# A third buffer for late outputs, and loads, stores and visits moved on one SyncE queue

## The chip, the cores and the metric

The kernel runs on one NeuronCore of one Trainium2 chip. The metric is the device time of one execution in microseconds; three unprofiled runs of the kernel before were taken, and one more execution with the hardware profiler, from which the trace comes.

## The reference

Windowed attention over 8 batches of 576 tokens, 8 heads of 64, followed by a dense softplus layer pair. Half of the heads see the last 32 keys, the other half every fourth of the last 128.

```python
scores = scale * np.matmul(q, k.transpose(0, 1, 3, 2))          # q, k, v: (8, 8, 576, 64)
mask_plain = (rel >= 0) & (rel < 32)
mask_dil = (rel >= 0) & (rel < 128) & (rel % 4 == 0)
attn = softmax(np.where(masks, scores, -1e9))
x = np.matmul(attn, v) as (4608, 512)
h = x @ w_in                                                     # (4608, 2048)
g = np.maximum(h, 0.0) + np.log1p(np.exp(-np.abs(h)))
return g @ w_out                                                 # (4608, 512)
```

## The kernel before

The 4608 tokens are nine chunks c of 512 columns. For each chunk the attention gives x (512 by 512), the first product gives h in 16 blocks ff of 128 rows, the softplus makes g, and the second product sums all 16 blocks into four PSUM banks o0 to o3 (m = 0 to 3). Every float32 operand is held as a high and a low part, so each product is three matmuls. Chunks 0 and 1 run in an opening stage written out as a list of words and in `slots` (one time unit is one slot: one block's h and one block's o). Chunks 2 to 8 run in a late stage: two blocks at a time take seven steps (`h_x`, `h_y`: a seven-product scheme on sums of x and weights), with about one quarter of a block's o between two steps. One round of seven steps is one `n`; its length in the trace is 10.55 us.

Attention of the chunks from 2 on is done two groups at a time, in visits that lie between the other PE work: `scores` (128 small matmuls into `s_ps`), then on DVE the maximum, on ACT the exponentials, on POOL the division, a DVE transposition `sq` that goes out to DRAM (`turned`) and comes back as `pt`, and then `values` (128 small matmuls into `a_ps` from `pt` and `v`). Its rows are turned by DVE, stored (`rows`) and read back as `x_full`.

The order is set by hand: `at(when, part)` puts a part at a time in slots, `step(n, k, part)` at a step of the late stage, and a heap hands them out; each engine then runs its instructions in the order in which they were written. `attend` places one visit of the opening stage, `attend_late(i)` visit i of eleven in the late stage, where scores come at step `begun` = 28i + 5 (plus `LATER_S[i]`) and values at `ended` = 28i + 28 + `LATER_V[i]`. Nearly all DMAs are issued by SyncE (SP, line 138) in the written order, and a DMA that has to wait holds back all behind it.

Two things touch DRAM beside loads and results. The opening stage leaves half-summed outputs of chunks 0 and 1 there (`kept`), which come back as `ob`. It also copies the 16 decoded blocks of `w_out` there (`keep_w_out`), since the SBUF that holds them is taken for other factors; the late stage loads them back, two 256 KB tiles `t` for each block.

`finished` closes a late chunk: for each m it copies the bank to one of the two halves of `ob` (m even on DVE, m odd on ACT) and stores that (`out_t`, 256 KB). So m = 2 takes the half of m = 0, and m = 3 that of m = 1. The bank is free for the next chunk's sum when its copy is done.

Of the kernel before, what the change touches and what calls it, by code (L numbers as in the profile page):

```python
# [14 lines left out]
F32 = mybir.dt.float32  # L15
# [9 lines left out]
P = 128  # L25
# [3 lines left out]
CH = 512  # L29
# [11 lines left out]
NPR = H // 2  # L41
# [4 lines left out]
FIRST = 2  # L46
# [49 lines left out]
def tile_windowed_attention_softplus_ffn(  # L96
# [13 lines left out]
    const = ctx.enter_context(tc.tile_pool(name="const", bufs=1))  # L110
# [9 lines left out]
    slots, at = [], {0: 0, 1: 0}  # L120
# [10 lines left out]
    def pin(ins):  # L131

        tc.keep_in_program_order(ins)
# [3 lines left out]
    def load_dma(engine=None, **kw):  # L137
        ins = tc.keep_in_program_order((engine or nc.sync).dma_start(**kw))  # L138
        if engine is None and len(under_way) < THIN:
            if len(under_way) >= DEPTH:  # L140
                tc.add_manual_dep(
                    ins.ins,
                    under_way[-DEPTH].ins.name,
                    mybir.DependencyInfo(mybir.DependencyClass.Sync, mybir.DependencyReason.DATA),
                    reason="at most so many of the first loads under way",
                )
            under_way.append(ins)
# [54 lines left out]
    def matmul(**kw):  # L202
        tc.keep_in_program_order(nc.tensor.matmul(**kw))  # L203

    def bank(name, tag):
        return psum.tile([P, CH], F32, name=name, tag=tag, bufs=2 if tag == "h" else 1)
# [422 lines left out]
    def at(when, part, *what, cost=0.0):  # L629
        heapq.heappush(events, (when, next(serial), cost, part, what))  # L630
# [169 lines left out]
    for word in OPENING.split():  # L800
        name = word[:3] if word[0] == "D" and word[1] != "l" else word.rstrip("0123456789_")
# [105 lines left out]
    def load_w_out(u):  # L907
        if u < len(uses):
            loaded[u] = [rest(2 * (u % 3) + part) for part in range(2)]
            for part in range(2):  # L910
                load_dma(out=loaded[u][part].bitcast(F32), in_=w_out[uses[u][1], :, part])

    def attend(n, when, lag):

        at(when, scores, n, cost=-1.45)
        for e in range(2):
            g, then = groups[n + e], when + e
            at(then + 0.12, g.maximum, cost=1.34)
            at(then + 0.37, g.exponentials)
            at(then + 1.0, g.divisor, cost=0.36)  # L920
            at(then + 1.0, g.divide)
            at(then + 1.37, turn, n + e, cost=0.65)
            at(then + 1.5, send, n + e)
            at(then + 2.2, bring, n + e)
        at(when + 3.3, load_v, n + 1)
        at(when + 3.45, load_queries, n + 2)
        at(when + lag, values, n, cost=-1.45)
        for e in range(2):
            at(when + lag + 0.25 + 0.25 * e, groups[n + e].turn_rows, cost=0.65)
        at(when + lag + 0.7, groups[n].send_x)  # L930
        at(when + lag + 1.25, groups[n].bring_x)
        at(when + lag + 0.01, load_keys, n + 2)
        at(when + lag + 1.3, load_v, n + 2)

    def decoding(keys):

# [19 lines left out]
    for p in range(EARLY):  # L956
        early += [((20.5, 20.5, 20.5, 20.5, 22.5)[p], *chore) for chore in chores_of(p)]
    for ff in range(NFF):
        at(18 + 0.55 * ff, keep_w_out, ff)
    for j in range(2):  # L960
        attend(FIRST * NPR + 2 * j, 10.2 + 7.5 * j, 4.125)
    attend((FIRST + 1) * NPR, 26.7, 4.6)
    at(26.2, ob_tiles, 0, True)
    for n in range(4):
        at(26 + 0.2 * n, combine, FIRST, n, cost=0.69)
# [6 lines left out]
    def step(n, k, part, *what, cost=0.0, after=0):  # L972

        at(LATE + 2 * n + STEP * (k + 0.9) + 0.001 * after, part, *what, cost=cost)
# [13 lines left out]
                step(n, 1, split_low, c, name, cost=0.7)  # L988

    LATER_S = (1, 0, 0, 1, 0, 0, 0, -1, 2, 1, 0)  # L990
    LATER_V = (0, -1, 2, 0, 0, 0, 0, 0, 0, 0, 3)

    def attend_late(i):

        n = (FIRST + 1) * NPR + 2 + 2 * i
        begun, ended = 28 * i + 5, 28 * i + 28 + LATER_V[i]

        def by(k, part, *what, cost=0.0, after=0):
            step(*divmod(k, 7), part, *what, cost=cost, after=after)

        by(begun + LATER_S[i], scores, n, after=1, cost=-1.45)
        for e in range(2):
            g, then = groups[n + e], begun + 7 * e
            late = 0 if e else max(LATER_S[i], 0)
            by(then + 1 + late, g.maximum, cost=1.34)
            by(then + 2 + late, g.exponentials, after=3)
            late = late // 2
            by(then + 6 + late, g.divisor, cost=0.36)
            by(then + 6 + late, g.divide)
            by(then + 8 + late, turn, n + e, cost=0.65)  # L1010
            by(then + 8 + late, send, n + e, after=4)
            by(then + 11 + late, bring, n + e)
        by(begun + 17, load_v, n + 1)
        by(begun + 20, load_queries, n + 2)
        by(ended, values, n, after=1, cost=-1.45)
        by(ended, load_keys, n + 2, after=2)
        for e in range(2):
            by(ended + 1 + e, groups[n + e].turn_rows, cost=0.65)
        by(ended + 3, groups[n].send_x, after=3)
        by(ended + 6, groups[n].bring_x, after=3)  # L1020
        by(ended + 8, load_v, n + 2, after=2)

    chores = []
    for c in range(FIRST + 1, NCH):
        n = (c - 1 - FIRST) * NPAIR
# [12 lines left out]
    for i in range(11):  # L1038
        attend_late(i)
# [30 lines left out]

    banks = [bank(f"h_{n}", "h") for n in "xy"]
    temps = const.tile([P, 3, HALF], F32, name="temps", tag="xl11")
    outs = []
    hs = {}

    def product(p, name, x, b, first):
# [30 lines left out]
        step(n + 1, 5 if second else 2, g_low, i, cost=0.69)  # L1107

    def finished(m, c, src):
        dst = outs[0][:, m % 2]  # L1110
        if m % 2:
            pin(nc.scalar.copy(out=dst, in_=src))  # L1112
        else:
            pin(nc.vector.tensor_copy(out=dst, in_=src))
        load_dma(out=out[m * P : (m + 1) * P, c * CH : (c + 1) * CH], in_=dst)

    def late_o(u, m, half=None):
        c, ff = uses[u]
        gh, gl = ready[len(slots) + u]
        first, final = ff == 0, ff == NFF - 1  # L1120
        if first and m == 0:
            for k in range(NKT):
                o_ps[k] = bank(f"o_ps{k}", f"o{k}")
        cols = slice(0, CH) if half is None else slice(half * HALF, (half + 1) * HALF)
        ws = slice(m * P, (m + 1) * P)
        for j, (part, gg) in enumerate(((0, gh), (0, gl), (1, gh))):
            matmul(
                out=o_ps[m][:, cols], lhsT=loaded[u][part][:, ws], rhs=gg[:, cols],
                start=first and j == 0, stop=(final or u == len(uses) - 2) and j == 2,
                skip_group_check=half is not None,  # L1130
            )
        if half is not None:
            return
        if final:
            if not outs:
                outs.append(const.tile([P, 2, CH], F32, name="ob", tag=f"w{NFF - 1}_1"))
            at(now[0] + (1 + (m == 2)) * STEP, finished, m, c, o_ps[m], cost=0.0 if m % 2 else 0.69)
        if m == NKT - 1:
            load_w_out(u + 3)

    pending = [(o_part, i, m) for i in range(len(slots) - LAG, len(slots)) for m in range(NKT)]
    pending += [(late_o, u, m) for u in range(len(uses) - 1) for m in range(NKT)]

    def outputs(n):
# [21 lines left out]
    for n, (c, p) in enumerate((c, p) for c in range(FIRST, NCH) for p in range(NPAIR)):  # L1166
        u = 2 * n
        for k, (x, weights, b, first, to, temp) in enumerate(steps):
# [10 lines left out]
            while chores and chores[0][:2] <= (n, k) and behind + chores[0][2] < 0.4:  # L1179
                _, _, cost, chore = chores.pop(0)  # L1180
# [8 lines left out]
    for half in range(2):  # L1189
        ob = const.tile([P, NKT, HALF], F32, name="pt", tag=("s", "v")[half])  # L1190
        for m in range(NKT):
            late_o(len(uses) - 1, m, half)
            src = o_ps[m][:, half * HALF : (half + 1) * HALF]
            if m % 2:
                nc.vector.tensor_copy(out=ob[:, m], in_=src)
            else:
                nc.scalar.copy(out=ob[:, m], in_=src)
            cols = slice(at_out + half * HALF, at_out + (half + 1) * HALF)
            if half and m > 1:
                engine = nc.sync if m % 2 else nc.scalar  # L1200
                engine.dma_start(out=out[m * P : (m + 1) * P, cols], in_=ob[:, m])
            elif m % 2:
                nc.sync.dma_start(
                    out=out[(m - 1) * P : (m + 1) * P, cols].rearrange("(m p) n -> p m n", p=P),
                    in_=ob[:, m - 1 : m + 1],
                )
# [120 lines left out]
```

## Time and profile before

| | |
|---|---|
| unprofiled runs | 885.37, 880.83, 882.01 us; median 882.01 |
| profiled execution | 885.35 us; its span 883.6 us |
| mean granted TensorE clock | 0.980 |
| busy share of the span | PE 97%, PEld 84%, DVE 70%, ACT 60%, POOL 4% |
| DMA | 168.81 MB, mean 191 GB/s |
| median from issue to landing | `t` 3.2 us, `v` 4.5 us, `w_out` store 5.8 us, `out_t` 2.4 us |

PE is busy nearly all of the time, so what can be won lies in the few places where it stands still, and those have to be looked for one by one. "Busy" counts modelled ends of pipelined matmuls. In a timeline row, the bracket at the end tells how long the engine was idle before the row and what ended that; "issue" means that no semaphore of the profile did. The chain of waits names at each moment the work that the end of the program hung on.

### The profile page before, as it was taken

The numbers are of one execution on the slowest core, as the hardware profiler recorded it, in microseconds if no ns is written. First come the engines' busy times: TensorE is split into PE (matmuls) and PEld (weight loads), VectorE is DVE, ScalarE is ACT, GpSimd is POOL, SyncE is SP. The second block draws the span as 40 slices with busy tenths as digits, with TensorE's granted clock in tenths as the row PEclk, the third lists the DMA queues.
The fourth block names the chain that finished last, engine by engine and source line by source line (L and its number), as shares of the span: only waits on it lengthen the run. The fifth ranks groups of instructions, "written<-read, shape, count | busy, mean of one in ns | idle before, by whom it ended". The sixth has DMA issues, their size and how long they took to land.

```text
span 883.6 us, 22785 instructions
## 1 busy us (share of the span) xinstructions
PE 856.5 (97%) x9143; PEld 739.5 (84%) x9143; DVE 618.5 (70%) x1260; ACT 533.0 (60%) x1327; POOL 31.6 (4%) x34
## 2 busy tenths in 40 slices
PE   6799999999999999999999999999899999999998
PEld 4578888787888988888788988898789888899897
DVE  5598898887888886576655776576647675675444
ACT  5587778766565756466554656565646564465443
POOL 0000000000000100000000000000000000000000
PEclk6699999999999999999999999999999999999999
DMA  9849445782757476666665665655575765434223
GB/s 328 299 132 365 182 133 183 259 297 79 214 193 222 162 217 198 198 186 209 206 190 187 183 215 187 220 175 190 174 217 168 215 192 173 135 105 144 96 97 118
DMA packets 107305, 168.81 MB, mean 191 GB/s; under 512 B 11072, under 2 KB 41920, under 8 KB 107200
## 3 DMA queue, kind: packets, MB, share of 16 engines
q1 hardware_dynamic: 106480, 166.18, 57.9%
q8 instruction: 72, 1.18, 0.6%
q10 hardware_dynamic: 720, 1.18, 0.4%
q14 instruction: 33, 0.27, 0.1%
HBM read 132.71 MB, written 34.60 MB: 189 GB/s over the span
## 4 chain that ended last, share of the span: by engine, by line
PE 85%; DMA 5%; ACT 4%; DVE 3%; issue 2%; SPq 0%; POOL 0%; ACTq 0%; DVEq 0%; POOLq 0%
PE o_ps L203 40%; PE h_x L203 17%; PE h_y L203 13%; PE h_ps L203 7%; PE a_ps L203 3%; PE s_ps L203 3%; DMA out_t<-ob 2%; ACT s L421 2%; DMA t<-w_out 1%; DMA ob<-kept 1%; DMA raw<-w 1%; PE t_ps L450 1%; DMA v<-vp 0%; SPq L138 0%; ACT ob L1112 0%
## 5 line engine op out<-in xcount | busy, mean ns | idle before, releaser
L203 PE MATMUL o_ps<-gh,t 128*128 128x512 f32 (+1 forms) x904 | 344.0, 393 | 6.1 <-ACT ob L1112 6.1
L203 PEld LDWEIGHTS o_ps<-gh,t 128*128 128x128 f32 x904 | 170.7, 189 | 29.4 <-ACT ob L1112 7.8
L666 ACT ACTIVATE e<-hs 128x512 f32<-128x512 f32 x112 | 70.0, 625 | 187.4 <-DVE hs L1098 187.3
L203 PE MATMUL o_ps<-gl,t 128*128 128x512 f32 (+1 forms) x452 | 179.1, 396 | 0.0
L685 ACT CAST gh<-e 128x512 fp32r<-128x512 f32 x140 | 86.3, 617 | 58.1 <-DVE e L673 56.6
L691 DVE TENSOR_TENSOR gl<-e,gh 128x512 fp32r<-128x512 f32 x144 | 102.4, 711 | 8.6 <-ACT gh L685 8.0
L203 PEld LDWEIGHTS h_x<-a,parts 128*128 128x128 f32 x672 | 96.1, 191 | 10.5 <-DVE temps L1096 0.4
L203 PEld LDWEIGHTS h_y<-s,t 128*128 128x128 f32 x672 | 94.3, 188 | 10.1 <-DVE temps L1098 0.2
L203 PE MATMUL h_x<-a,parts 128*128 128x256 f32 x672 | 99.7, 285 | 0.0
L203 PE MATMUL h_y<-s,t 128*128 128x256 f32 x672 | 98.8, 283 | 0.0
L668 ACT ACTIVATE e<-e 128x512 f32<-128x512 f32 x144 | 91.1, 633 | 4.6
L667 ACT ACTIVATE e<-e 128x512 f32<-128x512 f32 x144 | 91.1, 632 | 4.6
L203 PEld LDWEIGHTS o_ps<-gl,t 128*128 128x128 f32 x452 | 86.9, 192 | 2.9 <-DVE gl L691 0.4
L203 PE MATMUL h_ps<-xh,parts 128*128 128x512 f32 x256 | 89.0, 403 | 0.1
L203 PE MATMUL o_ps<-gh,parts 128*128 128x512 f32 x256 | 87.5, 394 | 1.0 <-DVE ob L746 1.0
L1098 DVE TENSOR_TENSOR hs<-h_x,temps 128x256 f32<-128x256 f32 x112 | 47.3, 422 | 58.0 <-PE h_x L203 57.6
L421 ACT ACTIVATE s<-s,nm 128x64 f32<-128x64 f32 x224 | 74.8, 335 | 9.7 <-DVE nm L413 9.6
L1098 DVE TENSOR_TENSOR temps<-h_y,temps 128x256 f32<-128x256 f32 x112 | 47.3, 423 | 46.0 <-PE h_y L203 45.5
L673 DVE SCALAR_TENSOR_TENSOR e<-hs,e 128x512 f32<-128x512 f32 x112 | 76.3, 681 | 2.1 <-ACT e L668 1.8
L1096 DVE COPY temps<-h_x 128x256 f32<-128x256 f32 x56 | 23.7, 422 | 57.2 <-PE h_x L203 57.1
L203 PEld LDWEIGHTS h_ps<-xh,parts 128*128 128x128 f32 x256 | 49.1, 192 | 11.3 <-DVE e L673 1.1
L203 PEld LDWEIGHTS o_ps<-gh,parts 128*128 128x128 f32 x256 | 48.1, 188 | 12.0 <-DVE ob L746 1.7
(82 smaller groups left out, 1195.2 us busy)
## 6 DMA issues: line engine op xcount, KB each, us to landing
t<-w_out SPq DMA_DIRECT2D x224, 256.0 KB, 3.2
raw<-w SPq DMA_DIRECT2D x64, 256.0 KB, 5.6
v<-vp SPq DMA_DIRECT2D x28, 512.0 KB, 4.5
q<-qp SPq DMA_DIRECT2D x36, 256.0 KB, 5.0
w_out<-parts SPq DMA_DIRECT2D x16, 512.0 KB, 5.8
out_t<-ob SPq DMA_DIRECT2D x32, 256.0 KB, 2.4
turned<-sq SPq DMA_DIRECT2D x112, 64.0 KB, 2.4
pt<-turned SPq DMA_DIRECT2D x28, 256.0 KB, 2.8
```

Source lines behind the costliest of these rows:

```text
L203: tc.keep_in_program_order(nc.tensor.matmul(**kw))
L421: pin(nc.scalar.activation(out=self.blocks[:, t], in_=src, func=AF.Exp, bias=self.nm[:, t : t + 1], scale=1.0 / 8.0 if self.masked else 1. ...
L450: nc.tensor.transpose(out=self.turned_to[:, m * P : (m + 1) * P], in_=self.s[:, m * P : (m + 1) * P], identity=ident,)
L666: pin(nc.scalar.activation(out=e, in_=tiles[i], func=AF.Abs))
L667: pin(nc.scalar.activation(out=e, in_=e, func=AF.Exp, scale=-1.0))
L668: pin(nc.scalar.activation(out=e, in_=e, func=AF.Ln, bias=1.0))
L673: pin(nc.vector.scalar_tensor_tensor(out=e, in0=tiles.pop(i), scalar=0.0, in1=e, op0=ALU.max, op1=ALU.add))
L685: pin((copy or nc.scalar.copy)(out=gh, in_=ready[i]))
L691: pin(nc.vector.tensor_tensor(out=gl, in0=e, in1=gh.bitcast(F32), op=ALU.subtract))
L1096: pin(nc.vector.tensor_copy(out=dst, in_=src))
L1098: pin(nc.vector.tensor_tensor(out=dst, in0=src, in1=temps[:, temp], op=ALU.add))
```

## The change

- `finished` hands out three buffers in turn (`stores` counts copies over all chunks): the two halves of `ob` and a new tile `third`.
- `load_v` of a late visit comes at step `begun` + 40 in place of `ended` + 8, that is nine steps later (one or two more where `LATER_V` was negative, fewer where it was positive). In the third opening visit it comes 1.1 slots later.
- `keep_w_out` of blocks 4 to 15 comes at 22.4 to 26.8 slots instead of 20.2 to 26.25.
- `LATER_V` of late visits 1 and 9 is one step lower: their values come one step earlier.
- In the third opening visit, the first group's maximum and exponentials come a quarter of a slot later.

```diff
-    def attend(n, when, lag):
+    def attend(n, when, lag, wait=0.0):
...
-            at(then + 0.12, g.maximum, cost=1.34)
-            at(then + 0.37, g.exponentials)
+            late = 0 if e else wait
+            at(then + 0.12 + late, g.maximum, cost=1.34)
+            at(then + 0.37 + late, g.exponentials)
...
-        at(when + lag + 1.3, load_v, n + 2)
+        at(when + lag + (1.3 if n < (FIRST + 1) * NPR else 2.4), load_v, n + 2)
...
-        at(18 + 0.55 * ff, keep_w_out, ff)
+        at(18 + 0.55 * ff if ff < 4 else 22.4 + 0.4 * (ff - 4), keep_w_out, ff)
...
-    attend((FIRST + 1) * NPR, 26.7, 4.6)
+    attend((FIRST + 1) * NPR, 26.7, 4.6, 0.25)
...
-    LATER_V = (0, -1, 2, 0, 0, 0, 0, 0, 0, 0, 3)
+    LATER_V = (0, -2, 2, 0, 0, 0, 0, 0, 0, -1, 3)
...
-        by(ended + 8, load_v, n + 2, after=2)
+        by(begun + 40, load_v, n + 2, after=2)
...
     def finished(m, c, src):
-        dst = outs[0][:, m % 2]
+        turn = stores.setdefault((c, m), len(stores)) % 3
+        dst = outs[1] if turn == 2 else outs[0][:, turn]
...
                 outs.append(const.tile([P, 2, CH], F32, name="ob", tag=f"w{NFF - 1}_1"))
+                outs.append(const.tile([P, CH], F32, name="ob", tag="third"))
```

SP's queue where late chunk 3 ends, before: `x_full` is the attention's output coming back, `v` the next visit's load, `t` the two tiles of a block of `w_out`.

```order
L138 DMA x_full<-rows 128x1024
L138 DMA out_t<-ob 128x512
L138 DMA v<-vp 128x1024
L138 DMA out_t<-ob 128x512
L138 DMA t_2956<-w_out 128x512
L138 DMA t_3018<-w_out 128x512
L138 DMA out_t<-ob 128x512 x2
```

The same place in the changed kernel.

```order
L138 DMA x_full<-rows 128x1024
L138 DMA out_t<-ob 128x512 x2
L138 DMA t_2956<-w_out 128x512
L138 DMA t_3018<-w_out 128x512
L138 DMA out_t<-ob 128x512 x2
```

The load of `v` has left the space between the first two stores. It is the first `v` in the next piece of the changed queue, which begins one pair of `t` after the last store; `turned` and `pt` belong to the visit's two groups, and the second `v` to the second group.

```order
L138 DMA turned<-sq 32x4x128 x4
L138 DMA pt<-turned 128x512
L138 DMA t_2592<-w_out 128x512
L138 DMA t_2649<-w_out 128x512
L138 DMA v<-vp 128x1024
L138 DMA t_2956<-w_out 128x512
L138 DMA t_3018<-w_out 128x512
L138 DMA turned<-sq 32x4x128 x4
L138 DMA v<-vp 128x1024
L138 DMA pt<-turned 128x512
```

It moved past the first group's `turned` and `pt`, and comes one `t` pair ahead of the second group's.

SP's queue in the opening stage, from the second visit's squares to the read of the kept outputs, before (`w_out<-parts` are the copies).

```order
L138 DMA turned<-sq 32x4x128 x4
L138 DMA w_out<-parts 128x1024
L138 DMA pt<-turned 128x512
L138 DMA v<-vp 128x1024
L138 DMA q<-qp 128x512 x2
L138 DMA w_out<-parts 128x1024
L138 DMA k<-kpl 128x544 x2
L138 DMA mask<-msk 128x512
L138 DMA w_out<-parts 128x1024 x2
L138 DMA rows<-turned_x 64x4x128 x4
```

The changed queue from the same squares.

```order
L138 DMA turned<-sq 32x4x128 x4
L138 DMA pt<-turned 128x512
L138 DMA v<-vp 128x1024
L138 DMA q<-qp 128x512 x2
L138 DMA k<-kpl 128x544 x2
L138 DMA mask<-msk 128x512
L138 DMA w_out<-parts 128x1024
L138 DMA rows<-turned_x 64x4x128 x4
L138 DMA w_out<-parts 128x1024
L138 DMA x_full<-rows 128x1024
L138 DMA v<-vp 128x1024
L138 DMA w_out<-parts 128x1024 x8
```

No copy of `w_out` stands before `v`, `q` and `k` any more, and eight stand in a row, where five did, before the kept outputs are read.

## Rows read from the trace of the kernel before

**Rows 1.** PE's waits: engine, line, releaser: us in total, times, longest us.

```profile
PE o_ps L203 <- ACT ob L1112: 6.1, 4, 2.7
PE s_ps L203 <- issue: 5.3, 4, 2.6
```

**Rows 2.** PE timeline at two chunk ends: start us, us, instruction, [idle before <-releaser].

```profile
438.36 0.79 PE L203 MATMUL o_ps<-gh,t 128*128 128x512 f32 x1 [2.12 <-ACT ob L1112]
...
625.99 0.73 PE L203 MATMUL o_ps<-gh,t 128*128 128x512 f32 x1 [2.68 <-ACT ob L1112]
```

**Rows 3.** ACT timeline at the first of these chunk ends.

```profile
437.72 0.59 ACT L1112 COPY ob<-o_ps 128x512 f32<-128x512 f32 x1 [5.18 <-DMA out_t<-ob]
```

**Rows 4.** SP timeline at the end of chunk 2, then of chunk 3.

```profile
336.15 0.42 SPq L138 DMA_DIRECT2D v<-vp  x1
339.31 2.18 SPq L138 DMA_DIRECT2D out_t<-ob  x2
...
430.20 0.34 SPq L138 DMA_DIRECT2D out_t<-ob  x1
430.59 0.43 SPq L138 DMA_DIRECT2D v<-vp  x1
432.05 0.34 SPq L138 DMA_DIRECT2D out_t<-ob  x1
```

**Rows 5.** Landing of `out_t` stores, chunk 2's four, then chunk 3's.

```profile
DMA to landing us min/median/max: 2.0/2.7/3.2
...
DMA to landing us min/median/max: 5.6/5.7/5.7
```

**Rows 6.** Chain of waits in order of time: start us, us, what.

```profile
166.25 4.13 DMA v<-vp
187.71 6.25 DMA ob<-kept
...
411.12 1.39 PE o_ps L203 x6
449.96 1.39 PE o_ps L203 x6
460.51 1.39 PE o_ps L203 x6
484.92 1.39 PE o_ps L203 x6
...
610.31 1.39 PE o_ps L203 x6
637.65 1.39 PE o_ps L203 x6
```

**Rows 7.** Windows: stretch us, length, busy of each engine, clock, DMA share, GB/s.

```profile
438.36:441.77 3.41, 3.41 (x11) 3.02 (x12) 0.45 (x2) 3.28 (x6) 0.00 (x0) 0.50 0.48 172
```

**Rows 8.** PE timeline inside the scores visits of late visits 2 and 10.

```profile
332.63 0.60 PE L203 MATMUL s_ps<-k,q 64*32 64x64 f32 x36 [0.94 <-issue]
...
707.52 0.45 PE L203 MATMUL s_ps<-k,q 64*32 64x64 f32 x30 [1.36 <-issue]
```

**Rows 9.** DMA queues from 330.0 to 331.7 us: packets, MB, share.

```profile
q8 instruction: 1, 0.02, 3.6%
```

**Rows 10.** PE timeline at the second opening visit's values.

```profile
170.52 0.85 PE L203 MATMUL a_ps<-v,pt 64*32 64x64 f32 x64 [0.99 <-DMA v<-vp]
```

**Rows 11.** DVE timeline, first sum with the kept outputs.

```profile
208.52 0.69 DVE L746 TENSOR_TENSOR ob<-o_ps,ob 128x512 f32<-128x512 f32 x1
```

**Rows 12.** Late visit 1: `pt` of its second group, issue and landing.

```profile
L138 SPq DMA_DIRECT2D pt<-turned x1: 338/338/338, 314.4 to 314.4; - x1
...
DMA to landing us min/median/max: 3.6/3.6/3.6
```

**Rows 13.** PE timeline, late visit 1's values.

```profile
320.48 1.51 PE L203 MATMUL a_ps<-v,pt 64*32 64x64 f32 x128
```

**Rows 14.** Landing of all 23 `v` loads from 200 us on.

```profile
DMA to landing us min/median/max: 3.6/4.3/6.4
```

More of the change, by code (lines that the diff above doesn't have):

```diff
@@ L1072, in tile_windowed_attention_softplus_ffn @@
     temps = const.tile([P, 3, HALF], F32, name="temps", tag="xl11")
-    outs = []
+    outs, stores = [], {}
     hs = {}
```

## The prediction

> **What bounds the kernel now.** I read the page's busy shares first: PE is busy for 97% of the span, so time can only come from the places where PE stands still or runs slowly. The table of PE's waits [rows 1] lists them by releaser. The largest that repeats late in the program is a bank of the second product that waits for ACT's copy `ob`: 6.1 us in four waits. The timeline shows the two long ones, 2.12 and 2.68 us, at the first matmul of a new chunk's sum into bank o3 [rows 2]. ACT itself had been idle for 5.18 us before that copy, and what ended this was the landing of a store `out_t` [rows 3]. So the chain is: store of m = 1, then the copy of m = 3 into the same half of `ob`, then bank o3, then PE.
>
> Why the store is late is read on SP's timeline. At the end of chunk 3, the 512 KB load of `v` is issued 1.46 us ahead of the second store; at the end of chunk 2 it goes out 3.2 us before the first one [rows 4]. The stores take 5.6 to 5.7 us there and 2.0 to 3.2 us here, and chunk 2's end shows no wait of PE [rows 5].
>
> A stall costs more than its length. In the 3.41 us after the wait of 2.12 us, the granted clock is 0.50, that is 1.2 GHz, though PE was at 2.4 GHz up to the wait and is busy for all of the stretch [rows 7]. The whole loss is read from the chain, where one and the same point of a round of seven steps recurs [rows 6]. A round takes 460.51 - 449.96 = 10.55 us. From 460.51 to 484.92 there are two rounds, one values and one scores visit and no stall, so both visits cost 24.41 - 21.10 = 3.31. From 411.12 to 449.96 there are three rounds and both visits: 34.96 expected, 38.84 taken, 3.88 lost. From 610.31 to 637.65 there are two rounds and one visit: 22.75 expected, 27.34 taken, 4.59 lost.
>
> **The stores.** The third buffer lets m = 3 follow m = 0's store, which is issued at 430.20 and not at 432.05 [rows 4], and the load of `v` no longer stands between them. ACT is idle there, so the copy then runs when the bank's sum is done, and DVE and ACT do as many copies as before. Even at 5.7 us [rows 5] the store of m = 0 would land at 435.9, where PE came to wait at 438.36 - 2.12 = 436.24 [rows 2]; with the copy's 0.59 [rows 3] that would leave a wait of some 0.25 us. At 2.0 to 3.2 us there is none. I take all four waits away: 3.88 + 4.59 for the two long ones with their slow stretch, and 6.1 - 2.12 - 2.68 = 1.30 for the two short ones [rows 1], 9.77 us. The bounds: 8.8 (a quarter of a microsecond left each time) to 9.8.
>
> What the moved load then does: `v` goes out nine steps later, 9 × 10.55 / 7 = 13.6 us. A late visit takes its values 23 steps after `begun`, and the load now comes 12 steps after it, so 11 steps or 16.6 us are left, and 9 steps or 13.6 us in visit 1. The slowest of 23 loads landed after 6.4 us [rows 14]. On the queue it passes the `turned` and `pt` of the visit's first group and stands one pair of `t` ahead of the second group's. That is the one place with little room (below). I cost the move at nothing; if its cover were gone, each visit would wait. The same holds for the opening load moved by 1.1 slots, which has a whole visit in hand.
>
> **Two values visits one step earlier.** Inside the scores visits that follow late visits 1 and 9, PE waits 0.94 and 1.36 us with "issue" as the reason [rows 8]: no data was missing, the matmuls themselves were. In the stretch of the first of them the instruction queue moved one packet [rows 9]. A visit is a dense run of short matmuls, so I read this as a refill of PE's instructions that came late because two such runs and the refill between them follow closely. The move takes the values run away from the scores run by one step, 9 to 12 PE matmuls, and leaves the place of all other PE instructions unchanged. I take both waits away, 2.30 us; the bounds are 0 and 2.30, and nearer to the upper one since a step lasts longer than either wait.
>
> The Trainium skill, on the page "Runtime: NRT & Kernel Launch", section "Instruction fetch mechanics", says that an engine's instructions are refilled in blocks of 16 KiB and that crossing a block is mostly hidden. By it the two waits would not be the refill's and the move would give nothing back: 875.1 instead of 872.8 in the sum below.
>
> The earlier visit has to find its `pt`. In visit 1 it was issued at 314.4 and landed 3.6 us later, at 318.0 [rows 12]; values started at 320.48 [rows 13]. What the visit is moved past on PE is one `h_x` product and two parts of the second product, some 2.1 us if the 7 products and 8 parts of a round of 10.55 are of one length. So it starts at about 318.4, with 0.4 us left. The new cost is 0, up to half a microsecond if `pt` is a little later. The turning of its rows on DVE moves along and adds nothing.
>
> **The copies of `w_out`.** In the second opening visit PE waits 0.99 us in the midst of the values for `v` [rows 10], and the load's 4.13 us are on the chain [rows 6]. Two 512 KB copies stood close to it in the queue, and none does now. The gain lies between 0 and 0.99; I take half, 0.5. Against it, three more copies stand in a row before the kept outputs are read. That read ended at 187.71 + 6.25 = 193.96 [rows 6], and its first use is at 208.52 [rows 11]. Three more transfers of 512 KB, at `v`'s median of 4.3 us one after the other [rows 14], end at 206.9, still in time; at 6.4 us each they would end at 213.2, 4.6 us late. As transfers overlap I take 0, and keep 4.6 as a bound.
>
> **The maximum.** Two DVE instructions trade places with one softplus instruction of the same size. One instruction of that size takes 0.69 us [rows 11]; the bounds are -0.7 and +0.7, and I take 0, since the cast that comes earlier on ACT fills the time in which ACT would wait.
>
> **The sum.** 9.77 + 2.30 + 0.5 = 12.57 us off the profiled execution's 885.35 (span 883.6 and 1.75 around it): 872.8. That execution is 3.3 us above the median of 882.01. If the runs differ by the size of the store waits, which chance sets (1.30 us for two of them and 2.68 for one in the same execution), all runs of the changed kernel come near 872.8; if they differ elsewhere, the median comes to 882.01 - 12.57 = 869.4. I take 872, nearer to the first.
>
> **The rivals.**
> - *Only the stores' part comes true.* The "issue" waits stay or turn up in another visit, and `v` in the opening is no faster: 885.35 - 9.77 = 875.6, up to 878 with some of the copies' bound. For it: no semaphore shows what ended those waits. Against it: they occur in just the two visits whose distance changes.
> - *The load of `v` finds a new collision.* It now goes out shortly ahead of the second group's `turned` and `pt`, eleven times. If `pt` comes late by enough that each visit waits 0.8 us, 8.8 us of the gain are lost: 881. For it: the 0.4 us that are left in visit 1. Against it: the old neighbours of the load were no better off, and other visits have room.
> - *The same, slower than before.* The place is the start of the values in all eleven visits. To be slower by over 0.5%, 4.4 us, it must eat 17 us, 1.55 us in every visit, and every one of the waits could bring the half clock. At 2 us a visit the time is 872.8 + 22 = 895. `v` can hardly do it, with 13.6 us or more against a slowest landing of 6.4; it decides only if `pt` lands 1.55 us behind its place in every visit, where even a whole transfer of 4.3 us [rows 14] in front of it shows that much only in visits with under 2.8 us in hand.
> - *The third buffer does not do what it says*: m = 3 still waits, now for m = 0's store, because the `t` loads alone make stores slow. That leaves at most the 0.25 us above, four times, and is inside the forecast.
>
> **How the numbers follow.** The forecast, 872 with a range of its own of 868 to 875.5, has 0.72; only the stores' part (875.6 to 878) 0.16; a new collision with a time near 881 0.09; the slow end 0.03. A difference of 0.5%, 4.4 us, is about what a measurement of this kernel can tell from none: faster means below 877.6. All of the forecast and nearly all of the second case are (0.72 + 0.15), the rest of it and the third are the same (0.10), and 0.03 is slower. The range of 8 in 10 takes in both medians of the sum and the second case: 867 to 878.
>
> **What would show it.** Right: no wait of PE or ACT with `out_t` behind it at the chunk ends, no stretch at half clock between 50 us and the tail, four stores per chunk at 2 to 3.5 us, the rounds at 10.55 us throughout, and no "issue" wait in the scores visits. The waits of DVE at the kept outputs should stay as they are. Wrong: PE waiting at `a_ps` for `pt` or `v` in several late visits, new "issue" waits in visits that had none, or the kept outputs landing after their first use.

## The result and the profile after

The changed kernel takes 873.75 us in the median of four runs (871.47 to 875.76), the kernel before 883.15 beside it. The ratio is 0.9893 with an interval of 0.9855 to 0.9931, 9.4 us less; 872.0 was forecast, with a range of 867 to 878. The profiled execution takes 873.08 us with a span of 871.2, against 885.35 and 883.6.

PE's waits of the changed kernel (engine, line, releaser: us in total, times, longest) answer to [rows 1]:

```profile
PE s_ps L203 <- issue: 5.0, 5, 1.4
...
PE o_ps L203 <- DVE ob L746: 1.0, 1, 1.0
...
PE a_ps L203 <- DMA pt<-turned: 0.4, 1, 0.4
PE a_ps L203 <- DMA v<-vp: 0.3, 1, 0.3
```

The line of `o_ps` behind ACT's `ob` with its 6.1 us is gone. The line of `s_ps` behind "issue" is not: 5.3 us in four waits before, 5.0 in five now. PE's wait behind the sums with the kept outputs (`ob` L746) stays at 1.0, as the prediction said.

At the first of the chunk ends of [rows 2 to 4], ACT's two copies and then SP's issues now read like this:

```profile
429.95 0.57 ACT L1114 COPY ob<-o_ps 128x512 f32<-128x512 f32 x1
430.94 0.59 ACT L1114 COPY ob<-o_ps 128x512 f32<-128x512 f32 x1
```

```profile
428.70 2.18 SPq L138 DMA_DIRECT2D out_t<-ob  x2
432.32 0.81 SPq L138 DMA_DIRECT2D out_t<-ob  x2
441.74 0.43 SPq L138 DMA_DIRECT2D v<-vp  x1
```

The copy of m = 3 starts 0.4 us after that of m = 1 ends, where it had been idle for 5.18 us, and `v` goes out 9 us after the last store. ACT still waits for a store once, at a later chunk end; PE has no wait behind it:

```profile
790.76 0.59 ACT L1114 COPY ob<-o_ps 128x512 f32<-128x512 f32 x1 [1.96 <-DMA out_t<-ob]
```

The row for 50 to 869 us in the windows (stretch, length, busy of each engine, clock, DMA share, GB/s) shows no slow stretch any more, where [rows 7] had one:

```profile
50.00:869.00 819.00, 811.22 (x8347) 708.91 (x8345) 585.49 (x1184) 501.26 (x1197) 30.08 (x28) 1.00 0.58 189
```

PE's timeline has the rows that answer to [rows 10], [rows 13] and [rows 8] (the wait stands in brackets):

```profile
166.60 0.85 PE L203 MATMUL a_ps<-v,pt 64*32 64x64 f32 x64 [0.31 <-DMA v<-vp]
...
240.42 0.43 PE L203 MATMUL s_ps<-k,q 64*32 64x64 f32 x24 [1.43 <-issue]
...
317.30 0.85 PE L203 MATMUL a_ps<-v,pt 64*32 64x64 f32 x64 [0.39 <-DMA pt<-turned]
...
331.07 0.60 PE L203 MATMUL s_ps<-k,q 64*32 64x64 f32 x36 [1.12 <-issue]
...
696.13 0.45 PE L203 MATMUL s_ps<-k,q 64*32 64x64 f32 x30 [0.95 <-issue]
```

The wait for `v` fell from 0.99 to 0.31, visit 1 waits 0.39 for `pt`, and the two "issue" waits that the move of the values was to remove are there, 1.12 and 0.95 after 0.94 and 1.36, with a third one of 1.43 at 240 us. That third wait cannot be put down to one edit: it is there, 1.42 to 3.31 us long, in all seven profiles below that have no fillers, and two of those (both back; the stores' part alone) share no edit with each other. The profile of the kernel before is the only one of these nine without it.

The two profiled executions differ by 12.27 us, close to the 12.57 of the sum, but not by the sum's terms. One more pair of rows is needed, the scores of the same opening visit, before and then after:

```profile
144.57 1.51 PE L203 MATMUL s_ps<-k,q 64*32 64x64 f32 x128
```

```profile
141.33 1.51 PE L203 MATMUL s_ps<-k,q 64*32 64x64 f32 x128
```

The changed kernel is 3.24 us ahead there already, and most of it before the first copy or load that the change moves. From there, with PE's matmuls of the two traces paired in their order, the lead grows by 3.89, 1.01, 4.48 and 0.82 us at the four chunk ends where the kernel before waits for `ob` (438 to 721 us), 10.2 together where the sum had 9.77, and by 0.68 at `v`; 1.20 are lost for "issue" (3.50 against 2.30) and 0.39 for `pt`. Together 12.5, some 0.3 more than the 12.27, which I do not place.

### The profile page after: what moved, and what is told of

Its sections match the earlier page's. It is cut to its first block, busy times and chain, and to the rows that moved or that the text cites. A ratio compares the mean times of both kernels' runs of the same rounds, so it can differ in the third digit from the quotient of the medians.

```text
span 871.2 us, 22769 instructions
## 1 busy us (share of the span) xinstructions
PE 850.1 (98%) x9143; PEld 736.1 (84%) x9143; DVE 618.5 (71%) x1260; ACT 533.7 (61%) x1327; POOL 31.1 (4%) x34
## 4 chain that ended last, share of the span: by engine, by line
PE 85%; DMA 6%; DVE 4%; ACT 2%; issue 1%; SPq 1%; POOL 0%; ACTq 0%; DVEq 0%; POOLq 0%
PE o_ps L203 41%; PE h_x L203 18%; PE h_y L203 13%; PE h_ps L203 7%; PE a_ps L203 3%; PE s_ps L203 2%; DMA v<-vp 2%; DMA turned<-sq 1%; ACT s L421 1%; SPq L138 1%; DMA k<-kpl 1%; DMA k<-kdl 1%; DMA raw<-w 1%; DMA q<-qp 1%; DMA pt<-turned 0%
```

## The experiments

The theory: the stores carry nearly all; the third buffer and the place of `v` each do the same job; the "issue" waits have to do with the blocks in which PE's instructions arrive, not with the distance of the two dense runs. The rivals: only one of the two parts counts for the stores; the "issue" waits come from that distance (the prediction), or from data that stands in front of the refill on DMA. Each run is compared with runs of the kernel before on the same chip.

**Without the third buffer.**

```diff
-        turn = stores.setdefault((c, m), len(stores)) % 3
-        dst = outs[1] if turn == 2 else outs[0][:, turn]
+        dst = outs[0][:, m % 2]
```

> The changed kernel with the copies of m = 2 and m = 3 again sharing the two halves of ob (m = 3 follows m = 1's store); the load of v stays away from the chunk ends. If the third buffer carries the gain of the stores, the waits of a bank for ob return at the chunk ends, 0.5 us and more in several of them, with a half-clock stretch after those of about 2 us, and the time goes back by up to 9.8 us, towards 883. If it is v's place in the queue that made the stores late, the stores of m = 1 land within 2 to 3.5 us, a wait is at most about 0.3 us, and the time stays at 873 to 875.

875.53 us, ratio 0.9918 (0.9890 to 0.9947); PE has no wait for `ob` at all, though ACT's copies still wait for stores, 9.1 us in five waits, the longest 2.65. The stores of the chunk's end at 434 us land quickly (landing of the four, from the view of `out_t`):

```profile
DMA to landing us min/median/max: 2.2/2.9/3.8
```

Moving `v` is enough by itself: paired with the kernel before, PE gains the same 10.2 us at the four chunk ends as the changed kernel does. The profiled execution is the slowest of five, 879.01: its scores of the same opening visit stand at 145.32, 4 us later, and a wait for issue at 246 us takes 3.31; neither has to do with the buffer.

**`v` back.**

```diff
-        by(begun + 40, load_v, n + 2, after=2)
+        by(ended + 8, load_v, n + 2, after=2)
```

The opening load goes back to 1.3 as well.

> The changed kernel with the load of v put back where it was, just ahead of the stores of m = 0 and m = 1 at some chunk ends; the third buffer stays. If the third buffer is enough, stores may take 5 to 6 us again, yet no bank waits for ob longer than about 0.3 us, and the time stays at 873 to 875. If v's place is what counts, waits of 0.5 to 2 us stay and the time goes back by 4 to 9 us. The waits for pt in visit 1 (0.35 us) should go if v's load in front of pt made them, and stay if the earlier visit alone did.

874.23 us, ratio 0.9909 (0.9894 to 0.9923). The stores are slow again, the slowest at the chunk's end at 612 us (the trace has the landings of two of its four):

```profile
DMA to landing us min/median/max: 5.3/5.3/5.3
```

ACT's copy waits for a store only this long:

```profile
431.46 0.59 ACT L1114 COPY ob<-o_ps 128x512 f32<-128x512 f32 x1 [0.17 <-DMA out_t<-ob]
```

and PE not at all. So the third buffer is enough by itself too, again with 10.2 us at the four chunk ends. The values of visit 1 do not wait for `pt` here. That wait shows in two of the nine profiles that have both the earlier visit and `v` ahead of `pt` (0.39 and 0.17), and in none of the others; whether the load makes it is not shown.

**Both back** (the two edits above together).

> The changed kernel without the third buffer and with the load of v where it was: what is left of the change is the copies of w_out, the values visits and the maximum. By the sum of the prediction the waits for ob return with their slow stretches, +9.8 us, so about 882 to 883. If most of the measured gain came from elsewhere (the start, the opening visits), the time stays below 879. Against the kernel before it says what the three small parts give together: 2.8 us by the prediction, 0.5 us or less if the waits with the reason issue never went.

880.17 us, ratio 0.9978 (0.9961 to 0.9994): 6.4 us of the 9.4 are gone, 7.5 by the ratios. The three small parts together are left with 0.5 to 3.4 us, so the run does not tell the 2.8 of the prediction from much less. The waits return; here are PE's sum over the run, then ACT's copy, PE's two long waits, and the window behind the second:

```profile
PE o_ps L203 <- ACT ob L1113: 4.3, 3, 2.7
```

```profile
436.34 0.59 ACT L1113 COPY ob<-o_ps 128x512 f32<-128x512 f32 x1 [4.28 <-DMA out_t<-ob]
```

```profile
436.98 0.50 PE L203 MATMUL o_ps<-gh,t 128*128 128x512 f32 x1 [1.22 <-ACT ob L1113]
...
622.71 0.50 PE L203 MATMUL o_ps<-gh,t 128*128 128x512 f32 x1 [2.70 <-ACT ob L1113]
```

```profile
622.71:626.20 3.49, 3.49 (x21) 3.13 (x22) 1.79 (x4) 3.36 (x6) 0.00 (x0) 1.00 0.64 212
```

The window's clock is 1.00. The wait of 2.68 in [rows 2] was followed by a stretch at 1.2 GHz and this one, as long and at the same place, was not. So the slow stretch is no fixed price of such a wait. By the pairing PE gains 5.2 us here at the four chunk ends against the kernel before, where the changed kernel gains 10.2: what the stores cost differs between executions.

**The stores' part alone**, put into the kernel before (third buffer and both moves of `v`).

```diff
-        by(ended + 8, load_v, n + 2, after=2)
+        by(begun + 40, load_v, n + 2, after=2)
...
-        dst = outs[0][:, m % 2]
+        turn = stores.setdefault((c, m), len(stores)) % 3
+        dst = outs[1] if turn == 2 else outs[0][:, turn]
```

> The kernel before with the third buffer and both moves of v's load, and nothing else of the change. By the sum of the prediction the stores alone give 9.77 us of the profiled execution, so about 873.5 against 882.4. The run with these two parts undone came to 880.2 and the changed kernel to 873.8 to 874.2, a difference of 6 to 6.5 us: if that is the stores' whole worth, this run comes to about 876, with no wait for ob at a chunk's end and the wait for v in the second opening visit still at 1 us.

876.24 us, ratio 0.9904 (0.9873 to 0.9935), 8.5 us less than the kernel before by the ratio and 8.0 by the medians; no wait of PE for `ob`, and again 10.2 us gained at the four chunk ends. The ratios of the whole change and of this part lie within each other's intervals.

**The copies of `w_out` evenly spread.**

```diff
-        at(18 + 0.55 * ff if ff < 4 else 22.4 + 0.4 * (ff - 4), keep_w_out, ff)
+        at(18 + 0.55 * ff, keep_w_out, ff)
```

> The changed kernel with the copies of w_out evenly spread again. If they made the values of the second opening visit wait for v, that wait comes back from 0.3 to about 1 us and the time rises by 0.7 us, which is less than the runs differ by; the trace decides. If the wait stays at 0.3 us, it was v's place (the moved load) and not the copies.

876.68 us, ratio 0.9907 (0.9883 to 0.9932), no difference in time that is clear of the noise. The wait comes back half way, in this run and in the one before it, which has the copies in the old places too:

```profile
168.37 0.85 PE L203 MATMUL a_ps<-v,pt 64*32 64x64 f32 x64 [0.47 <-DMA v<-vp]
```

```profile
168.26 0.85 PE L203 MATMUL a_ps<-v,pt 64*32 64x64 f32 x64 [0.59 <-DMA v<-vp]
```

With the copies moved it is 0.28 to 0.36 in the six profiles without fillers (0.28 and 0.36 in the two with `v`'s load back in its old place, so the load is not the reason), with them in place 0.47, 0.59 and 0.99. The term of 0.5 has the right sign and size, but two runs with fillers (below) show 1.50 and 0.82 with the copies moved: the landing of this one load swings by more than the copies do.

**The values visits back.**

```diff
-    LATER_V = (0, -2, 2, 0, 0, 0, 0, 0, 0, -1, 3)
+    LATER_V = (0, -1, 2, 0, 0, 0, 0, 0, 0, 0, 3)
```

> The changed kernel with the two values visits back on their steps. By the theory of the prediction the waits for issue in the scores visits (1.12 and 0.95 us in the changed kernel) get longer, 0.9 and 1.4 us as in the kernel before or more, and the time rises by up to 2.3 us. If the distance of the two runs plays no part, these waits stay within the spread that they show in the runs so far (1.1 to 1.4 and 0.6 to 1.7 us), the values of visit 1 wait no more for pt (0.35 us in the changed kernel), and the time stays within 0.5 us.

874.54 us, ratio 0.9896 (0.9848 to 0.9944). The wait for `pt` is gone, and the waits for issue are as in the kernel before:

```profile
332.08 0.60 PE L203 MATMUL s_ps<-k,q 64*32 64x64 f32 x36 [0.94 <-issue]
...
697.57 0.45 PE L203 MATMUL s_ps<-k,q 64*32 64x64 f32 x30 [1.38 <-issue]
```

These are the 0.94 and 1.36 of the kernel before. The first is 0.94 in all three profiles with the visits unmoved and 1.12 to 1.40 in the six with them moved, so the move seems to have lengthened it. The second is 1.36 to 1.65 unmoved and 0.62 to 1.72 moved. The prediction's reason for these waits falls.

**The rows' stores later.** Counting PE's records (matmuls, weight loads and the sequencer's semaphore waits) from the start, every wait for issue from the tenth microsecond on stands at one and the same place in a block of 256, number 193 (191 or 192 in four runs, whose traces lack one or two records), here and in every run that follows; the packets of the instruction queue are 72 of 16,384 bytes for 18,525 records, one for each such block. In the changed kernel's three waiting visits the packet starts 3.7, 5.1 and 4.1 us after PE has crossed the previous block's end, in most others 2 us before to 2.5 after. In the last two, stores of `rows` were in flight, so this run sends them later.

```diff
+        later = 6 if i in (1, 9) else 0
-        by(ended + 3, groups[n].send_x, after=3)
-        by(ended + 6, groups[n].bring_x, after=3)
+        by(ended + 3 + later, groups[n].send_x, after=3)
+        by(ended + 6 + later, groups[n].bring_x, after=3)
```

> The changed kernel with the stores of the turned rows (and the loads that bring them back) six steps, some 9 us, later after late visits 1 and 9 only, so that they go out behind the scores visit in which PE waits for issue (1.12 us at 329.95 and 0.95 us at 695.18). Theory A: the packet that refills PE's instructions stands behind the rows' packets; it then starts within 1.8 us of PE's crossing as in other visits, both waits go, and the time falls by about 2 us, unless the rows coming back later cost something. Theory B, that of the prediction: two dense runs close together make the refill late whatever else moves; both waits stay at about 1 us.

875.04 us, ratio 0.9922 (0.9894 to 0.9950), and both waits stay:

```profile
330.70 0.60 PE L203 MATMUL s_ps<-k,q 64*32 64x64 f32 x36 [1.12 <-issue]
...
695.90 0.45 PE L203 MATMUL s_ps<-k,q 64*32 64x64 f32 x30 [1.18 <-issue]
```

The previous block's end was crossed at 322.96. The windows from 324 us on, and then the DMA queues from 328.3 to 329.3 (packets, MB, share; q8 had none from 324 to 328.3), show that data did not hold the refill up:

```profile
324.00:326.00 2.00, 2.00 (x15) 1.83 (x14) 1.87 (x4) 0.09 (x1) 0.00 (x0) 1.00 0.00 0
326.00:328.30 2.30, 2.30 (x16) 1.91 (x14) 1.54 (x5) 0.00 (x0) 0.00 (x0) 1.00 0.67 227
```

```profile
q8 instruction: 1, 0.02, 5.8%
```

For two microseconds DMA was idle (share 0.00), and the packet came only behind the next pair of `t` loads. Theory A falls: what is late is the request, or whatever sets it off.

**All of PE's instructions moved by 128.** The fillers are one more loop at the start, once, where PE waits for `q` anyway:

```diff
+        for _ in range(64 if not shifted else 0):
+            matmul(out=unread[:, :64], lhsT=still[:, :P], rhs=still[:, :64], start=True, stop=True)
```

> The changed kernel with 64 more filler matmuls of 64 columns at the start, 128 instructions of TensorE with their weight loads; their output is not read. Every wait for issue so far stood at instruction 193 of a block of 256. If the waits belong to the ends of the blocks that are refilled, those at 238, 330 and 695 us vanish, since their visits are now crossed 128 instructions away (58 to 82 instead of 186 to 210 instructions into the dense run), and new ones may come where a dense run now holds a block's end at 180 to 210 instructions. If they belong to the visits themselves (their data, the load on DMA), they stay at about 1 us each. The fillers themselves cost 1 to 3 us at the start, unless TensorE waits there anyway.

871.14 us, ratio 0.9847 (0.9799 to 0.9895). The three old waits are gone, and two others are there, again at a block's end, now in visits that had never waited:

```profile
416.41 0.30 PE L203 MATMUL s_ps<-k,q 64*32 64x64 f32 x3 [1.13 <-issue]
...
508.87 0.48 PE L203 MATMUL s_ps<-k,q 64*32 64x64 f32 x33 [1.40 <-issue]
```

That settles where a wait can stand: at the end of a block. The old visits have their data and the distance of their runs as before and wait no more.

**By 40, a good place, and by 112, a bad one.** From the runs so far I made a rule: a dense run waits if a block's end falls 182 to 212 instructions into the scores, or more than 222 into any run. The edits are the one above with 20 and with 56.

> The changed kernel with 20 filler matmuls of 64 columns at the start (40 instructions of TensorE) where the last run had 64. Theory: a dense run of 256 short instructions stalls if a block's end falls 182 to 212 instructions into the scores, or more than 222 into any run; moved by 40 instructions, none of the 28 runs after 90 us has it there. Then no wait for issue over 0.3 us is left after 90 us (the changed kernel has three, 3.5 us), and the time falls by 2 to 4 us from 873.8, as far as the start (where dense runs follow one another) stays as it is. If places in the program stall for other reasons, waits of about 1 us stay or turn up elsewhere.

> The changed kernel with 56 fillers of 64 columns at the start, a shift of 112, chosen as a bad one. By the theory of the blocks' ends waits for issue come at about 97 (1.2 us), 223 (1.2), 467 (0.7), 512 (1.2), 556 (1.2) and 594 us (0.8), 6.3 us together, and none at 238, 330 and 695 us. If the theory is wrong, most of these places show none.

With 20: 872.81 us, ratio 0.9879 (0.9850 to 0.9907); none of the late dense runs waits for issue, as expected, but the fall of 2 to 4 us is not shown: it is 0.9 by the medians, with intervals that overlap. One wait of 0.6 us is new, in the second product just behind a run at 557 us, and `v` in the opening made PE wait 1.50 us. With 56: 873.9 us in a single run, and the rule fails. Six waits of 6.3 us were expected and two came, one of them at an expected place:

```profile
421.45 0.39 PE L203 MATMUL h_x<-s,parts 128*128 128x256 f32 x1 [0.71 <-issue]
...
513.23 0.43 PE L203 MATMUL s_ps<-k,q 64*32 64x64 f32 x25 [1.59 <-issue]
```

The place of the block's end decides where a wait can be, not that there is one. What makes the refill of some blocks late stays open.

**Two shifts, and a costly slip.** 64 fillers at the start and 84 ahead of a tile at 198 us, which stand all later runs as with 40.

```diff
+        for _ in range(84 if kt == 0 and i == len(slots) - 4 else 0):
+            matmul(out=tiles[i][:, :64], lhsT=win[:, 0, ws], rhs=win[:, 0, :64], start=True, stop=True)
```

> The changed kernel with 64 fillers at the start, as in the run whose start was 4 us shorter, and 84 more (168 instructions) ahead of a tile of the first product at 198 us, just before a wait of 0.95 us for the kept outputs. Their output is overwritten. After that all runs stand as with a shift of 40 (296 is 40 more than 256). Theory of the blocks' ends: the start stays short, the waits for issue at 415, 507 and 546 us (2.8 us) vanish and no others come; the fillers take some 0.9 us, hidden by that wait or not: 868 to 870 against 871.1. Otherwise: 871 to 874, with other waits for issue.

882.30 us, ratio 0.9994 (0.9972 to 1.0015). The visits' waits went, as expected (one of 0.88 us came in the second product), but the 84 fillers cost 14.6 us and not 0.9. Their groups (count: min/median/max ns, first and last start) and then two windows, early and late among them, say why:

```profile
L203 PEld LDWEIGHTS h_ps<-parts x84: 188/333/334, 199.8 to 214.5; 128*128 128x128 f32 x84
L203 PE MATMUL h_ps<-parts x84: 192/401/403, 200.0 to 214.6; 128*128 128x64 f32 x84
```

```profile
199.80:203.30 3.50, 3.50 (x32) 3.46 (x31) 1.66 (x5) 2.26 (x5) 0.00 (x0) 1.00 0.00 0
206.00:210.00 4.00, 4.00 (x21) 4.00 (x20) 3.09 (x7) 2.40 (x13) 0.41 (x1) 0.50 0.45 153
```

I had priced them by the visits' matmuls, which load 64x32 weights. A filler with its load of 128x128 came every 0.11 us at first, and the loads fill the window, so the 84 would have taken some 9 us at the upper clock (an estimate from the first window). While PE did only this the granted clock fell to 0.50, and from then on one came every 0.21 us. The last run changes the fillers' shape alone.

```diff
-            matmul(out=tiles[i][:, :64], lhsT=win[:, 0, ws], rhs=win[:, 0, :64], start=True, stop=True)
+            matmul(out=tiles[i][:32, :64], lhsT=win[:64, 0, :32], rhs=win[:64, 0, :64], start=True, stop=True)
```

> As the run with 64 fillers at the start and 84 at 198 us, but the 84 with weights of 64 rows and 32 columns, the shape of the visits' matmuls, of which 128 with their loads take 1.29 us, and not of 128x128, whose loads took 188 to 333 ns each and slowed 14.6 us. If that was the whole loss, the 84 take 0.8 to 0.9 us, the granted clock stays at 1.00 there, no wait for issue over 0.9 us is left after 90 us, and the time is 868 to 871, 1 to 3 us under the run with the 64 alone (871.1). If a dense run of narrow matmuls costs clock or a refill of its own here, 872 to 876.

869.55 us, ratio 0.9847 (0.9816 to 0.9879), the lowest median of all. The clock holds, and no dense run waits for issue after 90 us (the second product does once, 0.6 us at 555 us). The fillers on PE's timeline, and the window:

```profile
202.02 2.88 PE L203 MATMUL h_ps<-parts 64*32 64x64 f32 x84
```

```profile
202.00:205.00 3.00, 3.00 (x86) 2.94 (x86) 1.44 (x4) 2.01 (x4) 0.00 (x0) 1.00 0.02 5
```

The 84 take 2.8 us and not 0.9: they follow each other every 33 ns, the visits' matmuls of the same shape every 10, and why is not tested. Some of it lies where the wait of 0.95 for the kept outputs had been, which is gone. This version is faster than the kernel before, with the interval clear of 1. Against the changed kernel its ratio is 0.9847 to 0.9893 with intervals that overlap, so the 4 us between the medians are not shown; the run with the 64 fillers alone has the same 0.9847, so what the 84 add is not shown either.

## Why the prediction was right, and which step failed

*The stores* were right in mechanism: rows of ACT, SP and PE changed as said, and they are the bulk of the change, 8.5 us alone and 6.4 to 7.5 taken away (0.9978 against 0.9893), where 9.77 stood. For the profiled execution the term was right in size, 10.2 by the pairing. (Not all of chunk 3's stores were as slow as [rows 5] reads: its last one landed after 2.1 us.) The term was read from that one execution, slow stretches of 9.77 - 6.1 = 3.7 us included; in the run with both edits undone the chunk ends cost 5.0 us more than in the changed kernel, with 4.3 of waits and no slow stretch. Whether it is too large for the median is not shown: the interval of the stores' part alone goes from 5.7 to 11.2 us. That the two edits are redundant was not in the prediction: it priced them as one, with "some 0.25 us" left for the buffer alone, and the run with `v` back showed 0.17 on ACT and none on PE.

*The values visits* were the step that failed: "I take both waits away, 2.30 us". They stayed, 0.94 and 1.38 with the visits back, 1.12 and 0.95 with them moved. The reading of the packet in [rows 9] as a late refill was right; that it was late because two dense runs stand close together was not, and the runs with fillers put the block's end in its place; why the refill of some blocks is late stays open. The price that was named for the earlier visit, up to half a microsecond for `pt`, came: 0.39.

The rule on the page "Runtime: NRT & Kernel Launch" of the Trainium skill, section "Instruction fetch mechanics", gave the better number for this step, nothing, and not for its reason: it says that crossing a block is mostly hidden, and here each of these waits stands at a crossing, up to 3.31 us long behind the opening's first 50 us. Most of the 72 crossings are hidden.

*The copies*, 0.5: 0.68 in the profile, 0.1 to 0.3 by the runs with the copies back. *The maximum and the moved load of `v`*, 0: nothing in the profile answers to either, apart from the 0.39 for `pt`, to which the load adds.

*The forecast of 872* was near the 873.75 in part by luck. The profiled execution before was slow at its start by 3.24 us, against the changed one, which no term named, and this made up for the 2.30 that never came and the 1.59 of waits that were added. The scores of that opening visit stand at 140.8 to 145.3 us in the nine profiled executions without fillers, so a start of one execution says little on a kernel. Of the rivals, "only the stores' part comes true", 875.6 to 878, had its mechanism right: the "issue" waits stayed. Of the signs that were named, "no wait of PE or ACT" behind `out_t` came for PE alone (ACT waits 1.96 us once), stores landed after up to 4.1 us and not 3.5, and the new "issue" wait at 240 us is one of the signs of being wrong.

## What to carry to other kernels

When a copy waits for a store, look for what stands ahead of the store in the queue as well as for one more buffer: here either cured it, and both together gave nothing more that could be measured. A wait of PE with no releaser inside a dense run of short matmuls is worth counting out in PE's own instructions; where it fell on the same number modulo 256 everywhere, moving stores or visits did not help, and instructions put where the engine waits anyway moved it, though others came elsewhere. Do not price a filler by its columns: 84 of 64 columns took 14.6 us with weights of 128x128 and 2.8 us with 64x32.

## What the runs showed of the hardware

- Waits inside dense runs stand at one fixed number of a block of 256 PE records, one packet of 16,384 bytes each, in all fourteen profiles; PE goes on some 1.2 to 1.6 us after the end of the packet.
- Where a block's packet starts repeats at some blocks and not at others: behind 323 us it came 68 to 70 records after the crossing in seven profiles and 135 or 137 in two, though the transfers around it differed, and in one of the seven DMA had been idle for 2 us; at the block of the wait at 240 us it came 2.5 to 5.7 us after the crossing in the same nine.
- After waits of equal length (2.68 and 2.70 us) the clock was at its lower level in one execution and at the upper in another.
- Back-to-back loads of 128x128 weights with 64 columns each, PE busy throughout, brought the granted clock to 0.50; the same number with 64x32 weights left it at 1.00 (14.6 and 2.8 us long).
